# A new opening for an FFT and channel-mix kernel: one x transfer per part, mu by TensorE, feature angles on GpSimd

## The chip, the cores and the metric

The kernel runs on one core of one Trainium2 chip. The metric is the time of one execution on the device in microseconds (us), on the slowest core; with one core that is simply its time. "Step n" below is one of 192 equal pieces of the main loop (24 for each batch). A part or half "lands" when the last of its transfer's completion counts has come in.

## The reference

```python
# x: (8, 3072, 256) float32; d_ff = 1024
X = np.fft.fft(np.fft.fft(x, axis=1), axis=2).real.astype(np.float32)

x_prev = np.concatenate([zeros(B, 1, D), X[:, :-1, :]], axis=1)
xk = mu_k * X + (1.0 - mu_k) * x_prev
xr = mu_r * X + (1.0 - mu_r) * x_prev
k = np.maximum(xk @ w_k, 0.0)
v = k * k @ w_v
r = 1.0 / (1.0 + np.exp(-(xr @ w_r)))
return (r * v).astype(np.float32)
```

## The kernel before

A batch of x has 3072 rows, numbered 64·n1 + r with n1 from 0 to 47 and r from 0 to 63. Each batch comes in as two halves h. A half holds r = 16h to 16h+15 on partitions 0 to 47 and r = 32+16h to 32+16h+15 on partitions 48 to 95; so partition 48·g + n1 needs 16 neighbouring rows of 256 numbers, one contiguous piece of 16 KB in float32 that the transfer turns into 8 KB of float16. Stage A sums over n1 with sine weights w_pm, stage D over the features, stage C finishes the transform, then come the difference to the previous row, the mix with mu, and the three products. The loads of x are issued from GpSimd, into two buffers.

Words used below: an "evacuation" is the copy of a TensorE result out of a psW or psV tile by ScalarE or DVE (VectorE). "Dummies" are the matmuls of `keep_busy` on a zero tile. A relu is ScalarE's step on the result of k; relu number n belongs to step n. The "small m" and "w_eo fixes" are short operations on the sine tables m and w_eo. A d_half or d item is a piece of stage D (written to g_all), a c item a piece of stage C (written to pq); k_products and the v tiles are the matmuls for k and v.

```python
    xh_pool = ctx.enter_context(tc.tile_pool(name="xh", bufs=2))
    # ...
    x_r = x.rearrange("b (n1 r) d -> b n1 r d", r=R)          # N1, R = 48, 64

    def load_part(b, h, n, q0, nq):
        for g in range(2):
            r0 = 32 * g + 16 * h + q0
            nc.gpsimd.dma_start(out=xh_t[b, h][48 * g:48 * g + 48, q0:q0 + nq],
                                in_=x_r[b, :, r0:r0 + nq, :])

    def load_xh(b, h):
        xh_t[b, h] = xh_pool.tile([96, 16, 256], FP16, name="xh")
        load_part(b, h, 1, 0, 16)

    def butterfly(b, h, e):                    # the reader that frees a buffer of x
        # ...
        V.tensor_tensor(out=eo_t[b, h][:, :, e], in0=xh[:, :, 0:128], in1=xh[:, :, 128:256],
                        op=ALU.subtract if e else ALU.add)
    # ...
    keep_busy(11)                              # dummy matmuls on a zero tile
    load_part(0, 0, 2, 0, 8)                   # the first batch comes in parts
    # ... iota, iota
    load_part(0, 0, 2, 8, 8)
    # ... iota x3
    load_part(0, 1, 2, 0, 8)
    load_part(0, 1, 2, 8, 4)
    load_part(0, 1, 2, 12, 4)
    # ...
    # the weights of stage A know which row group and which n1 a partition holds
    V.tensor_copy(out=pcol_f, in_=pcol_i)                      # partition number
    V.tensor_scalar(out=hi48, in0=pcol_f, scalar1=48.0, scalar2=None, op0=ALU.is_ge)
    V.tensor_scalar(out=n1f, in0=hi48, scalar1=-48.0, scalar2=pcol_f, ...)
    V.tensor_scalar(out=u48, in0=k1c_f..., scalar1=n1f, scalar2=1.0 / N1, ...)
    # ...
    def flat(b):                               # one small row of y through a transfer
        V.memset(y_t[b, "f"][0:1, 0:1], 0.0)
        nc.sync.dma_start(out=y_t[b][0:1, 1], in_=y_t[b, "f"])
    # ...
    def v_out(c, tb, n):
        o = o_pool.tile([P, 2, 256], FP32, ...)                # 3 buffers
        V.scalar_tensor_tensor(out=o..., in0=st["v"]..., scalar=16.0, in1=st["r", c]..., ...)
        for s in range(2):
            # ... dst: every 48th row
            eng.dma_start(out=dst, in_=o[64 * s:64 * s + 64, 0:n])   # eng: SyncE
    # ... the opening
    a_sum(0, 0, 0)
    a_sum(0, 0, 4)
    m_sine(0, NS1)
    keep_busy(3)
    a_sum(0, 0, 8)
    a_sum(0, 0, 12)
    m_swap(0, NS1)
    m_rest(0)
    loads()                                    # mu, weight gathers, x of batch 1
    m_angles(NS1, NSL)
    keep_busy(2)
    a_sum(0, 1, 0)
    # ... rest of stage A, D and C, then the main loop with its table of work by step
```

## Time and profile before

| | before |
|---|---|
| time, median of 4 runs (lowest to highest) | 458.59 us (457.86 to 458.94) |
| span of the profiled execution | 459.5 us |
| first real matmul, stage D, first relu | 5.85, 15.65, 24.22 us |
| packets of GpSimd's queue q0 | 4688 |

The prediction below shows the lines of the span, the busy times, the windows and the opening's timeline. The page's lines of packets, of the queue that carries x, and of the chain that ended last (percentages of the span by engine):

```profile
DMA packets 32972, 40.25 MB, mean 88 GB/s; under 512 B 4480, under 2 KB 30592, under 8 KB 31584
q0 software_dynamic: 4688, 14.42, 18.8%
PE 93%; ACT 3%; DMA 1%; POOL 1%; issue 1%; DVE 0%; another core or an unknown queue 0%; POOLq 0%
```

TensorE (PE) makes up 93% of the chain and transfers 1%, which is x(0) in the opening: after that the chain waits for no load or store.

### The profile page before, as it was taken

The numbers are of one execution on the slowest core, as the hardware profiler recorded it, in microseconds if no ns is written. First come the engines' busy times: TensorE is split into PE (matmuls) and PEld (weight loads), VectorE is DVE, ScalarE is ACT, GpSimd is POOL, SyncE is SP. The second block draws the span as 40 slices with busy tenths as digits, with TensorE's granted clock in tenths as the row PEclk, the third lists the DMA queues.
The fourth block names the chain that finished last, engine by engine and source line by source line (L and its number), as shares of the span: only waits on it lengthen the run. The fifth ranks groups of instructions, "written<-read, shape, count | busy, mean of one in ns | idle before, by whom it ended". The sixth has DMA issues, their size and how long they took to land.

```text
span 459.5 us, 9804 instructions
## 1 busy us (share of the span) xinstructions
PE 447.2 (97%) x4087; PEld 327.6 (71%) x4087; DVE 360.0 (78%) x532; ACT 358.8 (78%) x398; POOL 35.6 (8%) x67
## 2 busy tenths in 40 slices
PE   8879999999999999999999999999999999999996
PEld 4647777777777777777777777777777777676764
DVE  7779988987788877978698777888679855898453
ACT  4689898888877887888887888878887888666661
POOL 8831000000000000000000000000000000000000
PEclk9999999999999999999999999999999999999999
DMA  7894561626622274214722265212222221223223
GB/s 131 128 177 90 120 140 46 124 64 138 124 62 67 49 146 109 70 48 90 164 68 58 59 136 120 69 48 69 55 63 61 56 70 47 71 64 75 70 68 93
DMA packets 32972, 40.25 MB, mean 88 GB/s; under 512 B 4480, under 2 KB 30592, under 8 KB 31584
## 3 DMA queue, kind: packets, MB, share of 16 engines
q1 hardware_dynamic: 28080, 25.07, 21.9%
q0 software_dynamic: 4688, 14.42, 18.8%
q8 instruction: 32, 0.52, 0.5%
q10 hardware_dynamic: 160, 0.13, 0.1%
q14 instruction: 12, 0.10, 0.1%
HBM read 28.84 MB, written 25.17 MB: 118 GB/s over the span
## 4 chain that ended last, share of the span: by engine, by line
PE 93%; ACT 3%; DMA 1%; POOL 1%; issue 1%; DVE 0%; another core or an unknown queue 0%; POOLq 0%
PE psV L592 36%; PE psW L555 35%; PE psW L578 9%; PE psW L431 5%; PE psW L407 4%; PE psW L458 3%; DMA xh<-in_x_dram 1%; ACT rl L565 1%; ACT g_all L395 1%; PE psW L421 1%; POOL xh L106 1%; ACT a L395 0%; ACT L583 0%; ACT pq L395 0%; ACT m L287 0%
## 5 line engine op out<-in xcount | busy, mean ns | idle before, releaser
L565 ACT ACTIVATE rl<-psW 128x1024 f16<-128x1024 f32 x192 | 196.7, 1026 | 80.8 <-PE psW L555 80.4
L555 PE MATMUL psW<-x,wk 128*128 128x512 f16 (+1 forms) x776 | 197.4, 377 | 2.5 <-ACT rl L565 1.5
L592 PE MATMUL psV<-wv_sb,k 128*128 128x256 f16 x1536 | 198.6, 272 | 0.0
L571 DVE TENSOR_TENSOR k<-rl 128x2048 f16<-128x2048 f16 x96 | 117.4, 1224 | 62.5 <-ACT rl L565 61.8
L592 PEld LDWEIGHTS <-k 128*128 128x128 f16 x1536 | 143.7, 98 | 20.3
L555 PEld LDWEIGHTS <-wk 128*128 128x128 f16 x776 | 75.7, 98 | 53.3 <-issue 4.0
L602 DVE SCALAR_TENSOR_TENSOR o<-psV,r 128x512 f32<-128x512 f32 (+1 forms) x97 | 66.3, 684 | 22.9 <-PE psV L592 20.7
L523 DVE TENSOR_TENSOR x<-y,t 128x1536 f16<-128x1536 f16 (+1 forms) x70 | 61.8, 882 | 2.4
L395 ACT ACTIVATE a<-psW 128x768 f16<-128x768 f32 x62 | 49.6, 806 | 4.0 <-PE psW L421 2.1
L578 PE MATMUL psW<-wr,x 128*128 128x256 f16 x384 | 49.8, 273 | 0.0
L583 ACT ACTIVATE r<-psW 128x1024 f16<-128x1024 f32 x48 | 49.0, 1021 | 0.8 <-PE psW L578 0.8
L578 PEld LDWEIGHTS <-x 128*128 128x128 f16 x384 | 37.6, 98 | 14.4 <-issue 0.2
L395 ACT ACTIVATE g_all<-psW 128x1024 f16<-128x1024 f32 (+1 forms) x46 | 46.9, 1022 | 1.1 <-PE psW L431 1.1
L106 POOL DMA_DIRECT2D xh<-in_x_dram x38 | 19.7, 525 | 238.7 <-DVE eo L119 222.7
L431 PEld LDWEIGHTS <-a 128*128 128x128 f16 x384 | 25.1, 98 | 10.0 <-issue 0.2
L407 PEld LDWEIGHTS <-eo 96*128 96x128 f16 x416 | 23.4, 97 | 11.6
L119 DVE TENSOR_TENSOR eo<-xh 96x2048 f16<-96x2048 f16 x26 | 31.5, 1213 | 0.0
L395 ACT ACTIVATE pq<-psW 128x896 f16<-128x896 f32 (+5 forms) x33 | 28.7, 871 | 1.6 <-PE psW L431 1.1
L431 PE MATMUL psW<-w_eo,a 128*128 128x128 f16 x368 | 27.7, 219 | 0.0
L407 PE MATMUL psW<-w_pm,eo 96*128 96x96 f16 x416 | 26.3, 205 | 0.0
L458 PEld LDWEIGHTS <-g_all 128*128 128x128 f16 x459 | 17.8, 98 | 7.7 <-issue 0.7
L510 DVE TENSOR_SCALAR t<-d,mu_f 128x1536 f16<-128x1536 f16 (+1 forms) x38 | 20.6, 543 | 0.1
(106 smaller groups left out, 158.5 us busy)
## 6 DMA issues: line engine op xcount, KB each, us to landing
out_dram<-o SPq DMA_DIRECT2D x190, 128.0 KB
xh<-in_x_dram POOLq DMA_DIRECT2D x28, 384.0 KB
xh<-in_x_dram POOLq DMA_DIRECT2D x6, 192.0 KB
wv_sb<-in_moe_w_v_dram POOLq DMA_DIRECT2D x1, 512.0 KB
xh<-in_x_dram POOLq DMA_DIRECT2D x4, 96.0 KB
out_dram<-o ACTq DMA_DIRECT2D x2, 64.0 KB
out_dram<-o SPq DMA_DIRECT2D x2, 64.0 KB
y<-f SPq DMA_DIRECT2D x7, 3.4 KB
```

Of the source, the lines that this page charges most:

```text
L395: nc.scalar.activation(out=out_ap, in_=in_ap, func=AF.Copy)
L407: nc.tensor.matmul(out=ps[:, 128 * i:128 * i + 96], lhsT=eo[:, 8 * j + i, e, :], rhs=w_pm[0:96, 0], start=True, stop=True)
L431: nc.tensor.matmul(out=_v(ps, 256 * i + 64 * (1 - e), [(128, 2), (1, 64)]), lhsT=a_t[b][:, e, 2 * u:2 * u + 2, :], rhs=w_eo[:, e, :], star ...
L458: nc.tensor.matmul(out=ps[:, o + 64 * i:o + 64 * i + 64], lhsT=g_all[:, u, col:col + 128], rhs=m[:, sl] if sl != 1 else mz[:, 0 if m is m1 ...
L523: V.tensor_tensor(out=dst, in0=_v(y_t[b], 64 * (NSL * a + lo + 3 * m), [(1, n)]), in1=_v(x_t["t", a], 64 * lo, [(1, n)]), op=ALU.subtract ...
L555: nc.tensor.matmul(out=st["k", ds][:, 512 * hs + lo:512 * hs + hi], lhsT=wk_sb[m][a][:, 128 * fc:128 * fc + 128], rhs=xk[:, a, 512 * i + l ...
L565: nc.scalar.activation(out=st["rl"][:, 2 * ds:2 * ds + 2], in_=st["k", ds].rearrange("p (f t) -> p f t", f=2), func=AF.Relu, bias=0.0, sca ...
L571: V.tensor_tensor(out=k2_t[c][:, 2 * ds - 2:2 * ds + 2], in0=r, in1=r, op=ALU.mult)
L578: nc.tensor.matmul(out=ps[:, 256 * tb:256 * tb + 256], lhsT=x_t[b, 1, m][:, a, 512 * i + 128 * tb: 512 * i + 128 * tb + 128], rhs=wr_sb[m] ...
L583: nc.scalar.activation(out=st["r", c], in_=ps, func=AF.Sigmoid)
L592: nc.tensor.matmul(out=st["v"][:, 256 * h:256 * h + 256], lhsT=k2_t[c][:, fc, 128 * tb:128 * tb + 128], rhs=wv_sb[:, fc], start=(fc == 0), ...
L602: V.scalar_tensor_tensor(out=o.rearrange("p a b -> p (a b)")[:, 0:256 * n], in0=st["v"][:, 0:256 * n], scalar=16.0, in1=st["r", c][:, 256 ...
```

## The change

It wants an earlier saturation of TensorE: x in one transfer for each part, so that GpSimd issues sooner; the columns of mu from contiguous rows by TensorE instead of by 4-byte loads and gathers; small angle work moved from DVE to GpSimd; a longer first sine; stage A's evacuations shared between ScalarE and DVE; a new order of the first 20 steps. The diff, cut to its core:

```diff
-    NS1 = 9
+    NS1 = 17
 ...
-    def load_part(b, h, n, q0, nq):
-        for g in range(2):
-            r0 = 32 * g + 16 * h + q0
-            nc.gpsimd.dma_start(out=xh_t[b, h][48 * g:48 * g + 48, q0:q0 + nq],
-                                in_=x_r[b, :, r0:r0 + nq, :])
+    def load_part(b, h, q0, nq):
+        src = x_r[b, 0:1, 16 * h + q0:16 * h + q0 + nq, :]
+        nc.gpsimd.dma_start(
+            out=xh_t[b, h][:, q0:q0 + nq],
+            in_=dataclasses.replace(src, ap=[[32 * D, 2], [R * D, N1], [1, nq * D]]))
 ... mu in two rows, permuted by ScalarE, turned into columns
-            nc.sync.dma_start(out=mu_f[0:1, 0, i:i + 1], in_=mu[0:1])
-            nc.sync.dma_start(out=mu_f[1:65, 0, i:i + 1], in_=mu[1:129:2][0:64])
-            nc.sync.dma_start(out=mu_f[65:128, 0, i:i + 1], in_=mu[2:128:2])
-            gather(mu_f[:, 1, i:i + 1], mu, 1)
+        nc.sync.dma_start(out=mu_row[:, i], in_=mu.rearrange("(a b) -> a b", a=1))
+    def mu_turn():
+        ps = ps_v()
+        for a in range(2):
+            for i in range(2):
+                c = 2 * a + i
+                nc.tensor.matmul(out=ps[:, c:c + 1], lhsT=mu_p[:, a, i], rhs=one, ...)
+        V.tensor_copy(out=mu_f..., in_=ps[:, 0:4])
 ... feature angles (pd_f, ueo), w_eo fixes, tw, u128, mirrored mu: from V to nc.gpsimd
 ... the opening
-    a_sum(0, 0, 0)
-    a_sum(0, 0, 4)
-    m_sine(0, NS1)
-    keep_busy(3)
-    a_sum(0, 0, 8)
 ... (what came after the first sine, loads() with it, is cut here)
+    loads()
+    eo_sine()
+    a_sum(0, 0, 0)
+    a_sum(0, 0, 4)
+    keep_busy(1)
+    m_sine(0, NS1)
+    a_sum(0, 0, 8, "V")
     a_sum(0, 0, 12)
     m_swap(0, NS1)
-    a_sum(0, 1, 0)
-    a_sum(0, 1, 4, "V")
+    a_sum(0, 1, 0, "V")
+    a_sum(0, 1, 4)
+    mu_turn()
+    m_ends()
+    eo_rest()
 ... the main loop: work of batches 0 and 1 in steps 0 to 20 put later, for example
-    at(2, a_sum, 1, 0, 0)
-    at(5, a_sum, 1, 0, 4)
+    at(6, a_sum, 1, 0, 0)
+    at(6, a_sum, 1, 0, 4)
 ... v tile 0 at step 4 instead of 5
```

## The prediction

> **What bounds the kernel now.** I read the page's header and slice rows first, then the engines' busy time in windows, then the same windows for the dummy matmuls alone (the ones on a zero tile, line 142), then the timeline of the first 45 us.
>
> ```profile
> span 459.5 us, 9804 instructions
> PE 447.2 (97%) x4087; PEld 327.6 (71%) x4087; DVE 360.0 (78%) x532; ACT 358.8 (78%) x398; POOL 35.6 (8%) x67
> ```
> ```profile
> 0.00:10.00 10.00, 8.71 (x47) 4.98 (x48) 7.84 (x41) 4.25 (x6) 8.40 (x27) 1.00 0.76 123
> 10.00:20.00 10.00, 7.45 (x99) 5.87 (x98) 7.57 (x25) 5.85 (x10) 8.31 (x10) 1.00 0.78 118
> 20.00:30.00 10.00, 6.66 (x71) 4.49 (x70) 7.44 (x23) 8.18 (x10) 6.65 (x8) 1.00 1.13 178
> 30.00:40.00 10.00, 9.26 (x95) 6.65 (x93) 9.65 (x27) 9.97 (x12) 0.59 (x2) 1.00 0.47 84
> 40.00:50.00 10.00, 10.00 (x94) 7.23 (x92) 9.79 (x20) 8.49 (x11) 1.51 (x3) 1.00 0.94 174
> ...
> 100.00:150.00 50.00, 50.00 (x474) 37.06 (x472) 40.32 (x52) 40.92 (x46) 2.02 (x4) 1.00 0.42 91
> ```
>
> Columns are window, length, then busy PE, PEld, DVE, ACT, POOL, the granted clock, the DMA share and GB/s. From 40 us to 430 us TensorE is busy without a gap at full clock, so nothing done to another engine there can move the end. Before 40 us TensorE is idle for 1.29 + 2.55 + 3.34 + 0.74 = 7.9 us. The dummies add 5.77 + 1.72 + 0.41 = 7.9 us of busy time that computes nothing. So of the first 40 us only 24.2 us is real matmul work; 15.8 us is **the whole sum that a new opening can draw on**. A gain of 2% (9.2 us) would need more than half of it.
>
> The waits that make up this loss, in order:
>
> ```profile
> 1.18 4.87 PE L142 MATMUL psV<-zeros 128*128 128x512 f16 x11 [1.18 <-DVE zeros L136]
> ...
> 11.80 2.14 PE L421 MATMUL psW<-w_pm,xh 96*128 96x192 f16 x24 [1.29 <-DMA xh<-in_x_dram]
> ...
> 15.22 0.59 PE L142 MATMUL psV<-zeros 128*128 128x512 f16 x2 [0.62 <-ACT a L395]
> ...
> 20.29 1.03 ACT L395 ACTIVATE g_all<-psW 128x1024 f16<-128x1024 f32 x1 [0.92 <-PE psW L431]
> ...
> 21.22 1.24 ACT L287 ACTIVATE m<-rl,m_pi 128x1152 f16<-128x1152 int32 x1
> ...
> 24.22 1.96 ACT L565 ACTIVATE rl<-psW 128x1024 f16<-128x1024 f32 x2
> ```
>
> The first real matmul starts at 5.85 us, behind a chain of small DVE operations that builds w_pm (ready at 5.73). The second half of x(0) holds it at 11.80. Stage D starts at 15.65 after the last evacuations. Then ScalarE is the narrow engine: the first relu starts at 24.22 because two evacuations and the second part of the sine table (1.24 us) stand ahead of it in its queue. From there to 40 us ScalarE is busy 18 of 20 us in the windows above, with gaps of 1.1 and 0.4 us near 27 and 28.5 us.
>
> **What the skill says.** *ScalarE: Activation LUTs*, section "What ACT_TABLE_LOAD costs", gives a table load of about 1283 ns and an ACTIVATE of 186 ns + 0.833 ns per element, with about 93 ns more for a pointer bias. The trace agrees: 1.28 us for a load, 1.24 us for the 1152-column sine (0.279 + 0.960), 1.03 us for 1024 columns. *GPSIMD Engine Reference*, section "Engine selection", calls one-input work on GpSimd roughly line rate; the trace has 0.2 to 0.4 us for a 128x1 tensor_scalar there against 0.15 us on DVE. *Advanced Engine Details and Errata*, "VectorE Performance Modes", says that DVE's second SBUF port is shared with GpSimd and that they block each other; no wait in this trace isolates it. *DMA: Bandwidth & Descriptors*, "Anatomy of one DMA", has about 2.0 us fixed; here the first x transfer was issued at 1.24 and its last completion count came at 4.80.
>
> **The change, part by part.**
>
> *x parts as one transfer of 96 partitions instead of two of 48.* The pair costs GpSimd 1.18 and 1.06 us, a 128-row gather 1.0; I take 0.6 to 0.7 for the single one. But the DMA share is 0.99 between 5 and 10 us, so bytes set the landings: completion counts put the parts of half 0 at 5.65 and 8.46 and the first of half 1 at 11.66. With issue 0.4 us sooner each I expect about 5.2, 7.7 and 10.2, and all of x(0) near 12.5 instead of 13.6.
>
> *w_pm.* The iota it needs moves from 2.51 to about 2.1, but DVE's own memsets end at 2.5: the first real matmul starts at 5.7 (gain 0.15).
>
> *Feature angles to GpSimd, zeros of g_all to ScalarE.* Removed from DVE before 10.2 us: 0.15 + 0.48 + 0.65 + 0.14 = 1.4 us; one 0.29 mask stays, earlier. ScalarE gets one 1408-column copy (0.19 + 1.17 = 1.4 us), two tiny ones and the mu rows, in its idle time from 2.0 to 4.8. Free unless the mu rows land after 4.8.
>
> *First sine part 17 slots instead of 9.* m_angles 0.76 to 1.27, wrap 0.46 to 0.71, sine 0.78 to 1.19, swap 0.61 to 0.9. In return, the late sine falls from 1152 to 640 columns (1.24 to 0.81) and moves behind two relus. DVE: w_pm 5.65, mask, ast 7.25, angles 8.5, wrap 9.25; ScalarE's sine 9.3 to 10.5. Two of the stage A evacuations go to DVE (0.96 each against 0.81): DVE then runs 9.35 evacuation, 10.5 swap, 11.4 evacuation, mu copy, the small m fixes (about 0.95) and w_eo fixes (0.33) to 13.85, last evacuation 14.45. Two dummies (0.43) and stage D at 14.9 instead of 15.65: **gain 0.75**.
>
> *mu by TensorE.* Six 4-byte-row loads and two gathers (0.95 + 1.41 us of GpSimd) go; four one-column matmuls and a copy come, about 0.3 us. The gathers of weights come 2 to 3 us sooner, but k_products at 20.5 did not wait for wk, so this is only slack.
>
> *From stage D to the first relu.* Stage D halves 14.9 to 15.8; pq evacuations about 17.3 to 18.6; two d evacuations to 20.6; the c item of slots 9 to 16 now goes ahead of k_products, so these start about 21.0 (20.52 before, a loss) but ScalarE then does its pq and the first relu at about 22.7 instead of 24.22: **gain 1.5, including the 0.75**.
>
> *From there to saturation (step 7's relu, at 41.06 before).* ScalarE's pieces from 22.7: eight relus at 0.95 = 7.6, sine 0.8, two d halves 1.1, a d item 1.0, a pq 1.0, table load and sigmoid 2.3, two a evacuations 1.5: 15.3, giving 38.0 without a gap. TensorE: 26.3 us of real work lay before 42.08 in the old trace (42.08 - 7.9 - 7.9); plus a v tile 0.87, mu 0.3, less the a_item and c item put off (0.6): 26.8. Of this 6.4 (stage A) and 2.6 (D and C) are done by 21.0, so 17.8 remain: 38.8 without a gap. The old trace lost 4.3 us in the same stretch (21.6 us for 17.3); DVE's tasks there lose 1.6 us (u128 and tw), 1.15 (m fixes) and 0.3 (mirrored mu), all to GpSimd, and the early c item takes away the 1 us gap near 27 us. I allow 1.0 to 1.5 us of remaining gaps. So step 8 starts near 40 instead of 42.1, and the rest follows unshifted: **458.8 - 2.3 = 456.5 us**.
>
> **The rivals.**
> 1. *Nothing arrives.* The data of x(0) and the chain d, c, halves, mix, k stay as they are; k_products even start later, and v_tile 0 at step 4 waits for its square on DVE (my estimate: 28.5 us). For it: DVE is 97% busy from 30 to 50 us. Against: the relu queue is shorter and TensorE has other work there. It gives 458 to 459.
> 2. *GpSimd and DVE collide.* Some 25 small GpSimd operations now run beside DVE's two-input ones, and the x parts of half 1 are issued behind three of them, about 4.8 instead of 4.43. If each costs DVE 0.1 us and x slips 0.5 us, 2 to 3 us are lost: 458 to 460. Against: DVE has given away 3 us in that stretch, and the slots of the DMA queue are filled until 7.7 us.
> 3. *It goes better.* With nearly no gap after 21 us, and the k_products not held by the c item, step 8 starts at 38: 454 to 455.
>
> **Range and chances.** The sum is 2.3 us, made of differences of half a microsecond; each milestone is uncertain by about 0.5, the last stretch by 1.5. Rival 1 or 2 in full takes it to zero, rival 3 doubles it. The range is 454.3 to 458.7. More than 2% would need 9.2 of the 15.8 us, which x(0)'s landing alone (5.85 us of start, then a wait until 12.5) rules out nearly; a loss of 2% would need a new wait in the dense part. Chances: faster 0.03, within 2% 0.95, slower 0.02.
>
> **What would show it.** Right: dummies 17 instead of 22; first real matmul near 5.7; stage D near 14.9; first relu near 22.7; v_tile 0 near 29; windows from 40 us on at 10.00 of 10.00 for TensorE; idle plus dummy time before 42 us at 13 to 14 us instead of 15.8. Wrong: a wait of ScalarE's first sine for the mu rows; stage D not earlier than 15.6; a TensorE gap over 0.5 us after 42 us; v tiles waiting for squares longer than 1 us.

## More of the kernel before

`load_part` is used by all 16 halves of x, not by the opening alone.

The costliest waits (engine, output and line, what was waited for: total us, times, longest):

```profile
POOL xh L106 <- DVE eo L119: 222.7, 10, 43.9
ACT rl L565 <- PE psW L555: 80.4, 180, 0.7
DVE o L602 <- PE psV L592: 20.7, 30, 1.6
```

GpSimd waits long to issue the next x, until DVE has read the old one: x is early. The others wait briefly for TensorE.

## The result, and the profile after

The changed kernel takes **607.78 us** (median of 4 runs, 607.02 to 608.53) against 458.59 us. The ratio is 1.326 (interval 1.323 to 1.328). Here and below a ratio is the mean time of one kernel's fast runs over that of the other's fast runs of the same rounds, so not quite the ratio of the quoted medians. The prediction of 456.5 us, with 2% for "slower", was wrong.

The page of the changed kernel:

```profile
span 605.8 us, 9765 instructions
PE 475.6 (79%) x4090; PEld 340.2 (56%) x4090; DVE 356.6 (59%) x497; ACT 361.7 (60%) x407; POOL 35.9 (6%) x71
DMA packets 45068, 40.30 MB, mean 67 GB/s; under 512 B 16574, under 2 KB 42688, under 8 KB 43680
q0 software_dynamic: 17088, 14.47, 13.6%
PE 48%; DMA 40%; DVE 7%; POOL 2%; issue 1%; ACT 1%; SPq 0%; DVEq 0%; POOLq 0%
```

DVE and ScalarE are as busy as before (357 and 362 us against 360 and 359). TensorE has 3 more matmuls and 28 us more of busy time (its granted clock was 0.896 over this span, 0.998 over the one before), but 130 us are idle where 12 were. The chain of waits is now 40% transfers. The bytes are the same, yet q0 has 12,400 packets more, nearly all under 512 bytes, and the 16 engines are busy with q0 for 82 us each on average (13.6% of 605.8) instead of 86 (18.8% of 459.5): the transfers do not cost more engine time, so it must be spread differently, in time or over the engines.

Windows of the changed kernel (columns as in the prediction):

```profile
10.00:20.00 10.00, 0.30 (x3) 0.29 (x4) 0.00 (x0) 0.00 (x0) 4.34 (x8) 0.50 1.00 167
...
50.00:60.00 10.00, 0.00 (x0) 0.00 (x0) 1.84 (x3) 0.00 (x0) 0.00 (x0) 0.50 0.26 53
...
100.00:150.00 50.00, 20.98 (x206) 15.77 (x207) 19.32 (x26) 16.79 (x20) 0.72 (x1) 0.70 0.22 47
```

From 10 to 20 us TensorE, DVE and ScalarE stand nearly still; from 100 to 150 us, where TensorE was busy 50.00 of 50 us before, it is busy 20.98. The granted clock there is 0.70; in stretches shown below, in which TensorE works densely, it is 1.00.

The timeline shows the opening's one wait (start, length, instruction, then idle time before it and its releaser):

```profile
19.70 2.74 PE L442 MATMUL psW<-w_pm,xh 96*128 96x192 f16 x16 [14.10 <-DMA xh<-in_x_dram]
...
37.17 1.94 ACT L589 ACTIVATE rl<-psW 128x1024 f16<-128x1024 f32 x2 [0.41 <-PE psW L579]
```

The first real matmul is at 19.70 us instead of 5.85, and the first relu at 37.17 instead of 24.22. The list of transfers gives the reason (KB each, median us from issue to landing). First the kernel before, then the changed one:

```profile
xh<-in_x_dram POOLq DMA_DIRECT2D x28, 384.0 KB
```
```profile
xh<-in_x_dram POOLq DMA_DIRECT2D x14, 768.0 KB, 34.4
xh<-in_x_dram POOLq DMA_DIRECT2D x3, 384.0 KB, 18.3
```

The page of before has no landing time for x. The completion counts in its trace have the first two parts of 384 KB (each as a pair of transfers) complete at 5.65 and 8.46 us, issued from 1.24 us on. In the changed kernel the first 384 KB land at 19.65, 18.3 us after their issue, and a whole half takes 34.4 us.

The waits of the changed kernel show where the rest of the loss is felt:

```profile
POOL xh L105 <- DVE eo L119: 316.2, 9, 63.2
ACT rl L589 <- PE psW L579: 174.3, 182, 18.2
DVE o L626 <- DMA out_dram<-o: 64.7, 11, 8.9
...
DVE d L523 <- DMA y<-f: 36.7, 4, 17.4
...
DVE eo L119 <- DMA xh<-in_x_dram: 26.4, 1, 26.4
```

DVE waits 64.7 us for a buffer of `o` whose store to HBM is not done, 36.7 us for the small row `y<-f`, and only once (26.4 us) for x itself. The list of the kernel before has no wait for a store and none of DVE for x; for `y<-f` it has 0.4 us, once. The chain of waits in order of time has the same (start, length, what):

```profile
1.41 18.25 DMA xh<-in_x_dram
...
35.53 30.83 DMA wr<-in_moe_w_r_dram,row_i
...
128.26 20.66 DMA y<-f
...
166.39 22.88 DMA out_dram<-o
```

A transfer of 3.4 KB (`y<-f`) takes 20.66 us, a store of 128 KB 22.88 us (its median is 2.5 us), and a gather of weights 30.83 us. So transfers that the change did not touch are slow at some times. Which times? GpSimd issued halves of x at 115.64 and 154.78 us, and each was under way for some 34 us: `y<-f` ended at 128.26 + 20.66 = 148.92, the store at 166.39 + 22.88 = 189.27, just as those halves landed. Windows with a half of x under way throughout (the first two) and without one (the last three) show it for the whole core:

```profile
116.00:150.00 34.00, 18.64 (x193) 13.89 (x192) 13.08 (x20) 16.16 (x20) 0.36 (x1) 0.80 0.24 52
155.00:189.00 34.00, 28.11 (x238) 19.87 (x236) 19.88 (x24) 21.50 (x23) 0.50 (x1) 0.90 0.29 63
232.00:258.00 26.00, 25.01 (x209) 17.90 (x209) 21.73 (x26) 18.78 (x20) 0.00 (x0) 0.93 0.24 58
306.00:324.00 18.00, 18.00 (x167) 13.34 (x165) 16.12 (x20) 14.94 (x17) 0.00 (x0) 1.00 0.31 74
...
450.00:590.00 140.00, 140.00 (x1202) 101.68 (x1201) 103.09 (x129) 106.08 (x115) 0.00 (x0) 1.00 0.26 63
```

Without x under way TensorE is busy for the whole stretch in two cases and for 25.01 of 26 us in the third; with it, it is busy 55% and 83% of the time (71 to 80% in the four later stretches with x under way, in which two halves overlap). The DMA share is low in both (0.24 to 0.31): the 16 engines together have room, so what is short cannot be their sum.

### The profile page after: what moved, and what is told of

It is laid out like the page before. It is cut to its first block, busy times and chain, and to the rows that moved or that the text cites. A ratio compares the mean times of both kernels' runs of the same rounds, so it can differ in the third digit from the quotient of the medians.

```text
span 605.8 us, 9765 instructions
## 1 busy us (share of the span) xinstructions
PE 475.6 (79%) x4090; PEld 340.2 (56%) x4090; DVE 356.6 (59%) x497; ACT 361.7 (60%) x407; POOL 35.9 (6%) x71
## 3 DMA queue, kind: packets, MB, share of 16 engines
q0 software_dynamic: 17088, 14.47, 13.6%
## 4 chain that ended last, share of the span: by engine, by line
PE 48%; DMA 40%; DVE 7%; POOL 2%; issue 1%; ACT 1%; SPq 0%; DVEq 0%; POOLq 0%
PE psV L616 19%; PE psW L579 18%; DMA out_dram<-o 17%; DMA y<-f 10%; DMA xh<-in_x_dram 9%; PE psW L602 5%; DMA wr<-in_moe_w_r_dram,row_i 5%; PE psW L452 2%; DVE k L595 2%; DVE x L548 2%; PE psW L428 1%; PE psW L442 1%; DVE o L626 1%; PE psW L483 1%; DVE t L535 1%
## 5 line engine op out<-in xcount | busy, mean ns | idle before, releaser
L616 PE MATMUL psV<-wv_sb,k 128*128 128x256 f16 x1536 | 209.2, 281 | 44.6 <-DVE o L626 39.4
L579 PE MATMUL psW<-x,wk 128*128 128x512 f16 (+1 forms) x776 | 205.7, 388 | 27.1 <-DVE x L548 27.1
L616 PEld LDWEIGHTS <-k 128*128 128x128 f16 x1536 | 147.8, 100 | 71.4 <-issue 41.3
L626 DVE SCALAR_TENSOR_TENSOR o<-psV,r 128x512 f32<-128x512 f32 (+1 forms) x97 | 66.3, 684 | 106.4 <-DMA out_dram<-o 64.7
L579 PEld LDWEIGHTS <-wk 128*128 128x128 f16 x776 | 77.6, 100 | 82.7 <-issue 33.6
L602 PE MATMUL psW<-wr,x 128*128 128x256 f16 x384 | 54.2, 287 | 37.4 <-DVE x L548 24.1
L602 PEld LDWEIGHTS <-x 128*128 128x128 f16 x384 | 39.2, 103 | 55.0 <-DVE x L548 24.5
L548 DVE TENSOR_TENSOR x<-y,t 128x1536 f16<-128x1536 f16 x60 | 57.5, 958 | 2.1
L119 DVE TENSOR_TENSOR eo<-xh 96x2048 f16<-96x2048 f16 x26 | 31.6, 1214 | 26.4 <-DMA xh<-in_x_dram 26.4
L523 DVE TENSOR_TENSOR d<-y 128x1664 f16<-128x1664 f16 (+3 forms) x19 | 16.8, 884 | 36.9 <-DMA y<-f 36.7
L105 POOL DMA_DIRECT2D xh<-in_x_dram x19 | 14.2, 750 | 337.8 <-DVE eo L119 316.2
L442 PE MATMUL psW<-w_pm,xh 96*128 96x192 f16 x88 | 11.7, 309 | 14.1 <-DMA xh<-in_x_dram 14.1
## 6 DMA issues: line engine op xcount, KB each, us to landing
xh<-in_x_dram POOLq DMA_DIRECT2D x14, 768.0 KB, 34.4
xh<-in_x_dram POOLq DMA_DIRECT2D x3, 384.0 KB, 18.3
```

The costliest lines, as they stand in the source:

```text
L548: V.tensor_tensor(out=dst, in0=_v(y_t[b], 64 * (NSL * a + lo + 3 * m), [(1, n)]), in1=_v(x_t["t", a], 64 * lo, [(1, n)]), op=ALU.subtract ...
L579: nc.tensor.matmul(out=st["k", ds][:, 512 * hs + lo:512 * hs + hi], lhsT=wk_sb[m][a][:, 128 * fc:128 * fc + 128], rhs=xk[:, a, 512 * i + l ...
L602: nc.tensor.matmul(out=ps[:, 256 * tb:256 * tb + 256], lhsT=x_t[b, 1, m][:, a, 512 * i + 128 * tb: 512 * i + 128 * tb + 128], rhs=wr_sb[m] ...
L616: nc.tensor.matmul(out=st["v", tb - h][:, 256 * h:256 * h + 256], lhsT=k2_t[c][:, fc, 128 * tb:128 * tb + 128], rhs=wv_sb[:, fc], start=(f ...
L626: V.scalar_tensor_tensor(out=o.rearrange("p a b -> p (a b)")[:, 0:256 * n], in0=st["v", t0][:, 0:256 * n], scalar=16.0, in1=st["r", c][:, ...
```

## The experiments

**Theory A**: the pattern of the new source. The Trainium skill, *DMA: Bandwidth & Descriptors*, section "Why a DMA increments its semaphore by 16 and not by 1", says how many engines a transfer is given: the largest number k up to 16 that divides the sizes of the slowest dimension (not of size 1) of both access patterns, as the instruction carries them. The destination's is 96 partitions; the source's is now 2. So k would be 2 of 16. For the old pair, 48 and 48, it is 16. **Rival B**: one transfer of 96 partitions from GpSimd is slow as such, or so many descriptors in one issue are. **Rival C**: something else in the change (the gathers put ahead of x, GpSimd's small operations, a half clock after a gap). The expectations call theory A "Theory S", rival B "Theory B" or "blunt form" and rival C "Theory R"; their theories C, D, E and G, further down, are about the clock and the rest of the change, not about rival C. "Before" below is the median of the kernel before on the same chip. Runs with one time only are single runs, whose state is unknown.

### Which part of the change

`after_pairs` is the changed kernel with the old `load_part`, and nothing else undone:

```diff
-        src = x_r[b, 0:1, 16 * h + q0:16 * h + q0 + nq, :]
-        nc.gpsimd.dma_start(out=xh_t[b, h][:, q0:q0 + nq],
-            in_=dataclasses.replace(src, ap=[[32 * D, 2], [R * D, N1], [1, nq * D]]))
+        for g in range(2):
+            r0 = 32 * g + 16 * h + q0
+            nc.gpsimd.dma_start(out=xh_t[b, h][48 * g:48 * g + 48, q0:q0 + nq],
+                                in_=x_r[b, :, r0:r0 + nq, :])
```

> The changed kernel with one thing undone: each x part is again two transfers of 48 partitions. Theory S (spread): the loss is all in the x loads, because the new source pattern begins with a dimension of size 2 and so only 2 of the 16 DMA engines work on a part; then this run is near 456.5 us (my sum for the rest, 454 to 459), x parts land in about 2 to 3 us each, no wait for out_dram or y<-f. Theory R (rest of the change: GpSimd work beside DVE, new order of the steps): it stays above 550 us.

Measured: 461.3 us (459.94 to 461.5), before 458.04, ratio 1.006 (1.004 to 1.008). The loss is gone; the time misses the 454 to 459 us that I had expected for the rest of the change, which is taken up below.

`before_single` is the kernel before with the new `load_part` (the same edit the other way round):

> The kernel before with one thing taken over: the single 96-partition transfer with the size-2 outer dimension. Theory S: 590 to 620 us, an x part of 8 rows lands 17 to 19 us after its issue, a half of 16 rows in about 34 us. Theory R: within 1% of 458.6 us.

Measured: 612.53 us (2 runs), before 458.04, ratio 1.337 (1.333 to 1.342). The whole loss goes with this one transfer, in both kernels; rival C is out for the loss. In `after_pairs` a half lands 6.1 us after its issue:

```profile
xh<-in_x_dram POOLq DMA_DIRECT2D x28, 384.0 KB, 6.1
```

### Size of the transfer, or number of engines

`inter_96` keeps one transfer of 96 partitions but lays x out so that partition 2·n1 + g holds what was on 48·g + n1. Then the rows of partition m start at 32·m rows, a single evenly stepped dimension of 96. The weights of stage A follow:

```diff
-            in_=dataclasses.replace(src, ap=[[32 * D, 2], [R * D, N1], [1, nq * D]]))
+            in_=dataclasses.replace(src, ap=[[32 * D, 96], [1, nq * D]]))
-    V.tensor_scalar(out=hi48, in0=pcol_f, scalar1=48.0, scalar2=None, op0=ALU.is_ge)
-    V.tensor_scalar(out=n1f, in0=hi48, scalar1=-48.0, scalar2=pcol_f, ...)
+    V.tensor_scalar(out=hi_i, in0=pcol_i, scalar1=1, scalar2=None, op0=ALU.bitwise_and)
+    V.tensor_copy(out=hi48, in_=hi_i)
+    V.tensor_scalar(out=n1f, in0=hi48, scalar1=-1.0, scalar2=pcol_f, ...)   # 2 * n1
-    scalar2=1.0 / N1
+    scalar2=0.5 / N1
```

> The changed kernel with the x rows laid on the partitions as p = 2*n1 + g instead of 48*g + n1, so that the 96 source rows have one stride and the single transfer begins with a dimension of 96; the cosine table is built for that layout (one DVE operation more). Still one transfer of 96 partitions per part. Theory S: like the pairs or a little better, 454 to 458 us, since 16 divides 96. Theory B (a single big transfer of 96 partitions is slow as such, whatever its pattern): stays near 600 us.

Measured: 458.99 us (458.43 to 459.17), before 458.04, ratio 1.002 (1.001 to 1.004). A single transfer of 96 partitions and 768 KB is not slow: rival B is out. (The 454 to 458 us expected were missed by 1 us.)

```profile
xh<-in_x_dram POOLq DMA_DIRECT2D x14, 768.0 KB, 6.8
```

`inter_2` has the same layout, with the same addresses written as two blocks of 48:

```diff
-            in_=dataclasses.replace(src, ap=[[32 * D, 96], [1, nq * D]]))
+            in_=dataclasses.replace(src, ap=[[32 * D * 48, 2], [32 * D, 48], [1, nq * D]]))
```

> As the interleaved run, same bytes from the same addresses to the same partitions, but the source pattern is written as 2 x 48 rows instead of 96. Theory S: 590 to 620 us again, 17 to 19 us for a part. A theory that blames the jump in addresses between the two groups (32 rows apart inside, 48 n1 steps) gives the same time as the 96 form, since the addresses run on evenly here.

Measured: 458.62 us (2 runs), ratio 1.001 (0.999 to 1.003): **a miss** for theory A as I had written it. Its q0 line is that of `inter_96` (4320 packets), so the two ran the same transfer. 48 steps of 32 rows are just the step of the outer dimension, so the two dimensions can be folded into one of 96. I take it that they were folded before the transfer was formed; I did not look at the instruction. The run then had no outer dimension of 2, and tests nothing about the number of engines. The next two use layouts that cannot be folded.

`outer_6` puts the rows of m = i + 6·j on partition 16·i + j, so the source is 6 blocks of 16 with a step that does not continue from one block to the next; `outer_3` does it with 3 blocks of 32. The weights follow again:

```diff
-            in_=dataclasses.replace(src, ap=[[32 * D, 2], [R * D, N1], [1, nq * D]]))
+            in_=dataclasses.replace(src, ap=[[32 * D, A], [A * 32 * D, b], [1, nq * D]]))
+            # outer_6: A, b = 6, 16;  outer_3: A, b = 3, 32
-    hi48 = (p >= 48);  n1f = p - 48 * hi48;              scale 1 / N1
+    hi48 = m & 1;      n1f = 95 * (p & (b - 1)) + p - b * hi48;  scale 0.5 / b / N1
```

(The last two lines are shortened; they stand for the same few DVE operations on 128x1 tiles.)

> The changed kernel with the x rows on the partitions in another order (row number 2*n1 + g = i + 6*j on partition 16*i + j), so that one transfer of 96 partitions has a source pattern of 6 x 16 rows that cannot be merged into one stride. Theory S in its sharp form (the number of DMA engines is the largest number up to 16 that divides the slowest dimension of both sides): 6 engines, so a part of 8 rows takes a third of the 17 us of size 2, about 6 us, and a half of 16 rows 11 to 12 us; total between 458 and 475 us. A blunt form (two-dimensional source rows are slow as such): near 600 us.

> The same with 3 x 32 rows (i + 3*j on partition 32*i + j). Theory S sharp: 3 engines, a part 11 to 12 us, a half of 16 rows 23 us, total between 480 and 560 us. Blunt form: near 600 us.

Measured: `outer_6` 474.2 us and `outer_3` 539.44 us (one run each, before 459.98). First `outer_6`, then `outer_3`:

```profile
q0 software_dynamic: 7360, 14.43, 17.6%
xh<-in_x_dram POOLq DMA_DIRECT2D x14, 768.0 KB, 14.0
xh<-in_x_dram POOLq DMA_DIRECT2D x3, 384.0 KB, 9.5
```
```profile
q0 software_dynamic: 12224, 14.45, 16.0%
xh<-in_x_dram POOLq DMA_DIRECT2D x14, 768.0 KB, 23.8
xh<-in_x_dram POOLq DMA_DIRECT2D x3, 384.0 KB, 17.5
```

The four kernels of one layout family or the other give a curve. The estimate in the fifth column is worked out from the packets in the traces: a half is 96 packets of 8192 bytes at a median of 0.624 us, 60 us of engine time, over k engines.

| slowest dimension of the source | kernel | time us | half lands after us | 60 us / k | 4-byte packets on q0 |
|---|---|---|---|---|---|
| 2 | changed kernel | 607.8 | 34.4 | 30 | 13,216 |
| 3 | outer_3 | 539.4 | 23.8 | 20 | 8,352 |
| 6 | outer_6 | 474.2 | 14.0 | 10 | 3,488 |
| 96 (k = 16) | inter_96 | 459.0 | 6.8 | 3.7 | 448 |

The landing is the estimate plus 3 to 4.4 us each time. The number of 4-byte packets gives k a second time, exactly: 448 is 16 for each of the 28 transfers on q0, and what lies above it, divided by the 19 transfers of x, is 672, 416 and 160, which is (16 − k)·96/k for k = 2, 3 and 6. That is as if an engine that gets no x were given as many 4-byte packets as a used one gets rows. The packet records of the traces (no view of the profile shows them one by one) give k a third time: while a single half is under way, 16 packets of 8 KB start in 5 us in the changed kernel, 23 or 24 in `outer_3` and 45 to 50 in `outer_6`; times 0.624 us that is 2.0, 2.9 to 3.0 and 5.6 to 6.2 packets under way at once. A single packet is no slower than in the kernel before (a median of 0.625 us there), so the jump in the source's addresses does not slow the packets either. **Theory A is shown**: the transfer runs on k engines, and k is the skill's.

Both totals fell into the expected ranges, and so did the half of `outer_3` (23.8 us for 23). Three landings missed: the half of `outer_6` took 14.0 us (11 to 12 expected), its parts of 384 KB 9.5 us (6), and those of `outer_3` 17.5 us (11 to 12). For the last one the trace has a lead: their 4 KB packets took 0.47 us in the mean, with a median of 0.35, so 32 of them on each of three engines make 15 us, and from 10 to 20 us the DMA share was 1.23 to 1.28. So other transfers seem to have shared the engines in the opening; no run tests it.

### Where in the kernel the loss arises

`single_open` uses the new transfer for batch 0 only, `single_rest` for batches 1 to 7 only, both in the changed kernel:

```diff
+        if b == 0:      # single_open;   single_rest: if b > 0
             src = x_r[b, 0:1, 16 * h + q0:16 * h + q0 + nq, :]
             nc.gpsimd.dma_start(...)       # one transfer, source of size 2
+        else:
+            for g in range(2):
+                nc.gpsimd.dma_start(...)   # the old pair
```

> The changed kernel with its size-2 transfers for batch 0 alone, pairs for all later batches. Theory S: x(0) lands 12 to 15 us later than with pairs and nothing later is touched: 472 to 480 us.

> The reverse: pairs for batch 0, size-2 transfers for batches 1 to 7. Theory S: most of the loss stays, 585 to 600 us, since each half of 16 rows takes 34 us and two buffers cannot hide that.

Measured: 474.92 us and 597.84 us (one run each, before 459.7), so 15.2 and 138.1 us. Together 153 us, against 149.2 us for the changed kernel (607.78 − 458.59). So the opening, which the change is about and which I had looked at, has only a tenth of the loss; nine tenths come from loads that were hidden and are hidden no more. `single_rest` shows which waits carry them, against those of the changed kernel above:

```profile
POOL xh L106 <- DVE eo L125: 327.0, 10, 63.7
...
DVE o L632 <- DMA out_dram<-o: 68.7, 11, 9.0
...
DVE d L529 <- DMA y<-f: 38.4, 4, 17.7
```

The waits for stores (68.7 us) and for the small row (38.4 us) make 107 of the 138 us if nothing overlaps them; DVE waits for x itself once, for 25.2 us. Do the stores wait on the very engines that carry x? The packet records do not name the engine, but they show it by their times. In the changed kernel, from 133.65 to 148.70 us, with one half under way, exactly 48 packets of x and 48 of the queue of the stores (q1) start, and nothing else. They form two trains, 0.055 us apart, in which one packet of x (0.624 us, 8 KB) and one of q1 (at most 1 KB, 0.059 us or less) take turns; each starts within 0.02 us of the other's end. 21 of the 27 packets of `y<-f` are done by 129.9 us; the last six pass in these trains from 146.70 to 148.01 us, behind 34 packets of stores. So a store packet that is given to one of the two engines of x waits 0.62 us for each packet of x, while the other engines stand idle. The skill's page, section "Queues, rings and completion order", says that each engine takes turns between the queues that have work for it; this trace agrees. With two halves under way, some 32 packets of x start in 5 us in the changed kernel, up to 50 in `outer_3` and up to 90 in `outer_6`: 4.0, 6.2 and 11.2 busy engines, about two times k, as if each half had engines of its own.

### What the rest of the change is worth

With the transfer mended, does the remaining change do what I predicted for it? `before_again` is the kernel before, unchanged, for a second trace.

> The kernel before, unchanged, for a second trace: the profiled run of the first trace was 461.3 us where the timed runs are 458. I expect 457.5 to 459 us and a first relu some 2 us earlier than 24.2 us, that is, that the first trace fell in an unlucky opening; if the opening stands as in the first trace, the 3 us lie elsewhere.

Measured: 460.13 us, span 458.4; first relu at 23.81 us. My expectation that it would be some 2 us earlier than in the first trace missed: it was 0.4.

`before_inter` is the kernel before with the transfer and layout of `inter_96` only (the diff of `inter_96`, applied to the kernel before).

> The kernel before with the interleaved layout and one transfer of 96 partitions for each x part, nothing else of the change. Bytes and engines are as before, GpSimd issues each part some 0.5 us sooner and x(0) lands about 0.7 us sooner; 0 to 1 us faster than the kernel before. Against the run with the rest of the change (inter_busy) it gives what the rest of the change is worth: by my sum 2 us, by the first timings nothing.

Measured: 459.24 us (459.21 to 459.38), before 459.7, ratio 0.999 (0.997 to 1.001), within what was expected.

`pairs_busy` and `inter_busy` add dummy matmuls against a half clock. In `after_pairs` the third wait for x is 1.90 us long (from 9.67 to 11.57 us), and the clock granted from 13.64 to 20.47 us is a half.

```diff
 # pairs_busy (after_pairs)              # inter_busy (inter_96)
     a_sum(0, 0, 12)                         a_sum(0, 0, 12)
     m_swap(0, NS1)                          m_swap(0, NS1)
+    keep_busy(6)                       +    keep_busy(4)
     a_sum(0, 1, 0, "V")                     a_sum(0, 1, 0, "V")
                                             # ... after mu_turn():
                                        +    keep_busy(2)
```

> The changed kernel with pairs of 48-partition transfers, plus six dummy matmuls in the wait for the second half of x(0). In the run with pairs alone the granted clock fell to a half from 13.6 to 20.5 us, after TensorE had idled from 9.7 to 11.6 us and around 14 us. Theory C (the half clock costs those 2 to 3 us): 458 to 459.2 us, clock 1.00 up to the end, against 461.3. Theory D (the pairs are slower because GpSimd issues them later): 461 us again.

> The changed kernel with the interleaved layout, plus six dummy matmuls in its two waits for x (four before the second half of x(0), two after the mu matmuls), as many dummies as the kernel before had and one more. The interleaved run had a clock of 0.995 to 0.997 in its timed runs, the kernel before 0.997 to 1.000. Theory C (lost clock hides the gain): clock 0.999 or more and 456 to 457.5 us where the kernel before has 458.5. Theory E (the rest of the change gains nothing outside of the profiled runs): within 0.5 us of before_inter.

Measured: `pairs_busy` 461.39 us (460.84 to 463.17), before 459.98, ratio 1.004 (1.000 to 1.008); `inter_busy` 460.48 us (460.07 to 461.53), before 459.7, ratio 1.002 (1.000 to 1.004). The window from 10 to 20 us of `after_pairs`, then of `pairs_busy`:

```profile
10.00:20.00 10.00, 8.42 (x68) 7.33 (x69) 5.95 (x17) 4.94 (x7) 8.10 (x14) 0.68 0.81 113
```
```profile
10.00:20.00 10.00, 9.29 (x111) 7.16 (x109) 7.86 (x22) 5.41 (x8) 8.10 (x14) 1.00 0.85 129
```

The clock of this stretch went from 0.68 to 1.00 and the median stayed, on another chip. The timed runs say more. In `after_pairs` three runs at 0.990 took 461.18 to 461.5 us, the one at 0.997 459.94; in `pairs_busy` the one at 0.990 took 463.17, the three at 0.997 to 0.999 460.84 to 461.4. So within each kernel a run with the lower clock is some 1.5 to 1.8 us longer (few runs): theory C is right in part. But without it the pairs are still 1.9 and 1.4 us above before on their chips, which theory C does not explain; that theory D (later issue) does is not shown. `inter_busy`, whose starting point had no half clock, misses both of its theories: it gained nothing, and is 1.24 us slower than `before_inter` on the same chip.

Last, three kernels on one chip with 5 rounds: `before_inter_b` and `inter_96b` are the two of those names again, and `inter_order` moves DVE's small work behind the last evacuations of stage A:

```diff
     mu_turn()
-    m_ends()
+    keep_busy(2)
     eo_rest()
     a_sum(0, 1, 8)
     a_sum(0, 1, 12, "V", 2)
     a_sum(0, 1, 14, "A", 2)
-    m_angles(NS1, NSL)
-    keep_busy(2)
+    m_ends()
     # ... four d_half
+    m_angles(NS1, NSL)
     m_wrap(NS1, NSL)
```

> The kernel before with interleaved single transfers again, now on the same chip as the next two: 0 to 1 us faster than the kernel before.

> The changed kernel with interleaved single transfers again. In the traces its step 4 began 4.6 us ahead of before_inter, step 8 1.4 us and step 20 1.1 us ahead, and it needs 0.3 us more after step 190. Theory G (the lead is mostly work put off, and is given back by step 20): 0.5 to 1 us faster than before_inter_b. Theory E (nothing is left of it, or it is turned by lost clock): the same or up to 1 us slower, with a clock below 0.998.

> The same with another order at the end of stage A: DVE does the w_eo fixes and the last evacuation before the small m fixes, the late angles move behind the evacuations of stage D, and the two dummies stand in the wait after the mu matmuls instead of before stage D. In the trace TensorE stood still from 14.0 to 15.1 us for that evacuation. Expected: stage D starts at 14.6 to 15.0 us instead of 15.6, 0.4 to 0.8 us less than inter_96b in all; if the later evacuations of stage D on DVE take it back, the same time.

Measured, with 459.85 us for before: `before_inter_b` 459.24 us (459.11 to 459.40), ratio 0.998 (0.996 to 1.001); `inter_96b` 459.81 us (459.53 to 459.97 over its four fast runs), ratio 0.999 (0.996 to 1.003; its other two runs, at 467 us, are left out); `inter_order` 460.15 us (458.5 to 462.15), ratio 1.000 (0.996 to 1.003). No version beats the kernel before beyond the intervals. All four fast runs of `inter_96b` lie above all six of `before_inter_b`, by 0.6 us in the medians: beside the new transfer, the rest of the change costs a little rather than gains, so theory G missed. `inter_order` missed in its profiled run, where stage D started at 16.68 us and not at 14.6 to 15.0; the granted clock was a half from 12.87 to 19.70 us there. Its two runs at a mean clock of 0.992 took 461.72 and 462.15 us, the four others 458.5 to 460.5. Starts of relu number n in the traces tell where the lead goes:

| kernel (span us) | n = 0 | 4 | 8 | 20 | 100 | from 191's start to the end |
|---|---|---|---|---|---|---|
| before (459.5) | 24.22 | 33.06 | 43.14 | 72.76 | 252.40 | 10.53 |
| before_again (458.4) | 23.81 | 31.90 | 42.01 | 71.62 | 251.26 | 10.54 |
| before_inter (457.4) | 22.77 | 30.99 | 41.09 | 70.71 | 250.35 | 10.53 |
| inter_96 (456.6) | 22.38 | 27.69 | 39.65 | 69.63 | 249.27 | 10.78 |
| inter_96b (458.2) | 24.45 | 29.75 | 41.72 | 71.22 | 250.86 | 10.78 |
| after_pairs (459.7) | 25.52 | 30.84 | 42.80 | 72.77 | 252.41 | 10.76 |

`inter_96` leads `before_inter` by 3.3 us at relu 4, by 1.4 at relu 8 and by 1.1 at relu 20; the tail takes 0.25 more. `inter_96b` gives back the same 1.9 us between relu 4 and relu 8 (from a lead of 1.2 to a lag of 0.6). I take this to be the work of batch 1 that the change puts later, which TensorE must do after all; it was not measured apart. And one and the same program varies by 2 us in its opening from one execution to another (`inter_96` against `inter_96b`): its first relu came at 22.38 or at 24.45.

## Why the prediction was wrong

**The step that failed** is this one: "But the DMA share is 0.99 between 5 and 10 us, so bytes set the landings … With issue 0.4 us sooner each I expect about 5.2, 7.7 and 10.2, and all of x(0) near 12.5". It takes the rate of the transfers as given and prices only their issue. The first part landed at 19.65 us, because the new transfer ran on 2 of the 16 engines. The share of 0.99 could not rule that out: it adds up the packets of all transfers (1.13 from 20 to 30 us in the kernel before), and in the changed kernel it was 1.00 from 10 to 20 us, with the weights beside five parts of x, each on 2 engines. It says nothing on how many engines one transfer gets. I had cited the very page that has the rule, for its fixed 2.0 us, and not applied the rule to the line of the diff that writes a slowest dimension of 2. Mending the pattern alone (`inter_96`) takes 607.8 us back to 459.0.

**"Nothing done to another engine there can move the end"** was wrong too, from 40 us on. No run tests it for the compute engines alone, but x loads with 34 us instead of some 6, in two buffers, made stores, a small row and gathers wait. That is the 138 us of `single_rest`, and I gave "a new wait in the dense part" 2% because I looked for it among the instructions that the diff moves in time, not in a function that all 16 halves use.

**The sum for the rest** can be judged on `inter_96`. Dummies 17: they were 17. First real matmul 5.7: 5.79. Parts of x at 5.2, 7.7 and 10.2 and all of x(0) near 12.5: the completion counts stand at 5.74, 7.65, 10.31 and 12.24, so with 16 engines these terms were right. Stage D at 14.9: 15.56 here, 14.55 in `inter_96b`; but `before_inter`, with the transfer alone, has it at 14.40, so what was gained there was the transfer's. First relu 22.7: 22.38 in this execution, 24.45 in the other. The turn of mu "about 0.3 us": 1.05 us of TensorE, a term sized too small by 0.75 us. Step 8: relu 8 at 39.65, against 43.14 in the trace that I had read, so 3.5 us instead of the 2.1 (2.3 in the last line of the sum) that I had allowed. "The rest follows unshifted" failed by 0.6 us: at the end the lead over that trace is 2.9 (456.6 against 459.5).

The larger fault is the trace that the gain was counted from. Its execution took 461.26 us, a late opening, but I took the 2.3 us off the median of 458.8. Against `before_inter` the lead of `inter_96` is 1.4 us at relu 8 and 0.8 at the end. Nor is the profiled span of 456.6 us a hit of the predicted 456.5: that was a time, and the time of this run is 458.43 us, the best of its four; the median is 459.0, 0.95 above before's on that chip. **Rival 1**, "nothing arrives", 458 to 459, describes the mended change best; why it does not arrive (later work, openings that vary) is only partly what rival 1 had said. Rival 2's slip of x by some 0.5 us did happen in `after_pairs` (half 1 issued at 5.18 us, 4.43 before), where the time was 461.3 us.

**What stays open**: whether other transfers made the parts of `outer_3` late, why the opening of one program varies by 2 us, what makes the clock fall to a half in some runs, and where the pairs lose their last 1.4 to 1.9 us.

## What to carry to other kernels

When a diff rewrites the access pattern of a transfer, work out over how many engines it spreads before and after, from the slowest dimension of source and destination, and do this before pricing its issue: merging two transfers into one can leave it an eighth of the engines. Then ask who else calls the changed function: a load that was wholly hidden can, once slow, hold up stores and small transfers that nobody touched. Judge gains below 2 us by timed rounds and by two traces of the old kernel, not by one, and take a gain off the time of the execution in whose trace it was read.

## What the Trainium skill lacked or had wrong

- *DMA: Bandwidth & Descriptors*, "Why a DMA increments its semaphore by 16 and not by 1": the rule for k holds here. A half of 768 KB landed after 34.4, 23.8, 14.0 and 6.8 us with a slowest source dimension of 2, 3, 6 and 96. Lacking: a transfer on k engines comes with 4-byte packets, (16 − k)·96/k of them here for each transfer of 96 rows, 12,768 in the changed kernel, as if the engines left out got one for each row of a used engine. They make k readable from the packet count of a page.
- The same section says "as the instruction carries it", but not what becomes of the pattern as written: 2 blocks of 48 with an even step ran like one dimension of 96 (`inter_2`, 458.62 us, 4320 packets), while 2 blocks that do not continue each other took 607.8 us.
- The same page, "Rules for kernel authors": the advice of one transfer for two disjoint partition halves was worth a ratio of 0.998 to 0.999 here, within the intervals (`before_inter`, 459.24 us), and, followed without a look at the outer dimension, cost 1.326. Another row of the same table has the limit (an outermost dimension smaller than 16 confines a transfer to at most so many engines), but the row with the advice does not refer to it.
- None has it: no page that I read puts a number on what a transfer on few engines does to others: waits of 64.7 us for stores and 36.7 us for a 3.4 KB row in the changed kernel, against none and 0.4 us in the kernel before; on the engines of x one packet of 1 KB or less passed for each 8 KB packet of x, about every 0.66 us.
- *TensorE: Matmul & The Clock Gate*, "What's actually happening", lets the clock fall to a half after an idle window of about 3.4 us (a later section, "A second HAM failure mode: psum-queue depth-cycling", has frequent short gaps do it too, without a length). In `after_pairs` it was a half from 13.64 to 20.47 us though the longest idle stretch before was 1.90 us; with 6 dummies it stayed at 1.00 in the profiled run. The length of the gaps alone does not settle it here: `inter_order` had a half clock from 12.87 us on after gaps of at most 1.20 and 1.03 us, and `inter_96`, whose longest were 1.20 and 1.04 us, kept 1.00.
